# A fourth matmul group ahead of the first output, one product on GpSimd, and other unit widths, in an attention block fused with a mixture of experts

## Chip, cores and metric

The kernel runs on one core of a Trainium2 chip. The metric is the device time of one execution in microseconds; smaller is better. All data is float32 (the sketch matrices S1 and S2 arrive as float64 and are turned into float32 on the chip).

## What is computed

The first block is an attention with a sketched polynomial feature map; its output is the input x of a gated mixture of four experts.

```python
batch, n_heads, seq, head_dim = (4, 4, 1088, 32)   # r = 8
def phi(x):
    a = np.einsum('rd,bhsd->bhsr', S1, x)
    b = np.einsum('rd,bhsd->bhsr', S2, x)
    return np.einsum('bhsi,bhsj->bhsij', a, b).reshape(*x.shape[:-1], r * r)
q_p, k_p = (phi(q), phi(k))
kv = np.einsum('bhsf,bhsd->bhfd', k_p, v)
z = np.sum(k_p, axis=2)
num = np.einsum('bhsf,bhfd->bhsd', q_p, kv)
den = np.einsum('bhsf,bhf->bhs', q_p, z)[..., None] + 1e-06
x = num / den                              # laid out as 4352 rows of 128
...
p = domain_probs / (domain_probs.sum(-1, keepdims=True) + 1e-09)
for e in range(4):                         # F = 1024
    out += p[:, e:e+1] * (np.maximum(x @ w1[e], 0.0) @ w2[e])
```

## The kernel before

**Chunks and steps.** The 4352 columns of x (one per token, 128 partitions each, held in `xT`) are worked through in eleven chunks of 128, 448, 512 (six times), 320, 256 and 128 columns (`CHUNKS`; chunk 0 and the last are "plain"). A chunk has 16 steps, four for each expert, and steps are numbered through: step 16 is the first of chunk 1, step 48 the first of chunk 3. `first(i)` makes step i's hidden values: matmuls of `w1_sb` with `xT` into a bank `h` (three such banks, pool `ps_h`), a relu on ScalarE (ACT, L799 in a plain chunk, L807 otherwise) and, in chunks that aren't plain, rectify-and-subtract on VectorE (DVE, L778). Such a step has two halves j = 0 and 1, each with its own bank h, one L778 instruction in the first half and two in the second. `second(i)` multiplies the hidden values with the second weights into the banks `o0` and `o1`. The main loop issues `first(i)` and then `second(i - LA)` with LA = 2. After an expert's last step `gather` and `gather_rest` sum the output on ACT and GpSimd (POOL); `weight_sums` puts further sums on POOL up to step 28.

**Attention in pieces.** The attention of the 4 batches is cut into 275 pieces (`front`), which are put between the steps' halves by `work()`. A batch has first 19 pieces for its keys (`keys`: three turns kT, three projections kp0 to kp2 with copies by ACT, three copies of values by ACT together with the first of eight products `kp` on DVE (L383), two empty pieces, two key sums on PE, one block product), then 20 pieces for each unit of queries (`queries`: a turn qT, a projection qc into the bank `f`, shuffles and products on DVE giving qp, and `attend`: matmuls into the banks `den` and `num`, a reciprocal, a product xs, a turn y, and DMAs on SyncE's (SP) queue out to DRAM and back into xT). Units may have other widths than chunks; `UNITS` has them for each batch, and each batch has 1088 columns.

**Pacing.** `needed[m]` is the number of pieces after which all columns of chunk m have been issued. Before each step the rate of pieces is set to the largest over the chunks c ahead of

```python
(needed[c] + (8 if c > 1 else 4) - done[0]) / (START[c] - gone)
```

times the columns of a step. Each half adds half the rate to a credit, and a piece is issued for every whole credit.

**Start.** `start()` is written out by hand: keys of batch 0, the first unit of 128 columns by `attend_first` (banks `den` and `num`, into xT by L526), and the projection of the second unit. Key products there are shared between DVE (those with a `kf` argument read the bank in PSUM) and POOL (these read the copy `fs` in SBUF); key sums into `f`, `kvz` (L406) and the reciprocals follow. Then the h of steps 0 to 2 are begun on the first 64 columns of xT, while the second 64 are still made (`begun_hp`, `half_columns`).

Of the kernel before, what the change touches and what calls it, by code (L numbers as in the profile page):

```python
# [23 lines left out]
def kernel(  # L24
# [23 lines left out]
    nc = tc.nc  # L48

    P = 128  # L50
    HP = 64
# [10 lines left out]
    CW = 512  # L62
    GE = 160
    LA = 2
    UNITS = [[P, 448, 512], [512, 320, 256], [448, 512, P], [384, 320, 384]]

    CHUNKS = [P, 448, 512] + [512] * 5 + [320, 256, P]
    NC = len(CHUNKS)
# [10 lines left out]
    ps_n = ctx.enter_context(tc.tile_pool(name="ps_n", bufs=1, space=bass.MemoryType.PSUM))  # L79
# [3 lines left out]
    def psum(pool, tag):  # L83
        return pool.tile([P, 512], F32, tag=tag, name=tag)
# [217 lines left out]
    def load_gate(m, engine=nc.sync):  # L302
        gate[m] = mpool.tile([P, CW * E], F32, tag="gate", name="gate")
        for b, c, n, at in parts(m):
            engine.dma_start(
                gate[m][:, at * E : (at + n) * E], gates[b, c * E : (c + n) * E].partition_broadcast(P)
            )
# [72 lines left out]
    def key_product(b, t0, n, p, x, eng, kf=None):  # L380

        src, off = (kf, P * p) if kf is not None else (fss[b], 32 * (NT * p + t0))
        eng.tensor_tensor(  # L383
            out=_ap(kps[b], 0, P, 256 * t0 + P * p + 64 * x, [[256, n], [32, 2], [R, 4], [1, R]]),
            in0=_ap(src, 0, P, off + 4 * x, [[32, n], [R2, 2], [1, 4], [0, R]]),
            in1=_ap(fss[b], 0, P, 32 * (NT * p + t0) + R, [[32, n], [R2, 2], [0, 4], [1, R]]),
            op=ALU.mult,
        )
# [277 lines left out]
    def start():  # L666


        b, n = 0, UNITS[0][0]
        kf = []  # L670
        for t0 in (0, 2):
            key_turn(b, 0, t0, 2)
        for r in (1, 2):
            key_turn(b, r)
        qT = query_turn(b, 0, n)
        for gi in range(3):
            kf.append(psum(ps_h, "h"))
        value = value_copy(b)
        key_project(b, 0, kf[0])
        key_project(b, 1, kf[1])  # L680
        next(value)
        key_project(b, 2, kf[2])
        for _ in value:
            pass
        fq = [psum(ps_o, "o0"), psum(ps_o, "o1"), psum(ps_n, "num")]
        for i in range(3):
            for j in range(2):
                both(fq[i][:, 0:n], sr[:, i, j, :], qT[:, 0:n], start=(j == 0), stop=(j == 1))
        qb = apool.tile([P, QW], F32, tag="qb", name="qb")
        nc.scalar.copy(qb[:, 0:n], fq[0][:, 0:n])  # L690
        for x in range(2):
            key_product(b, 0, 4, 0, x, nc.vector, kf[0])
            key_product(b, 0, 4, 1, x, nc.gpsimd)
        for x in range(2):
            key_product(b, 4, 4, 0, x, nc.vector, kf[1])
            key_product(b, 8, 1, 0, x, nc.vector, kf[2])
        key_product(b, 4, 5, 1, 0, nc.gpsimd)
        key_product(b, 4, 4, 1, 1, nc.vector, kf[1])
        key_product(b, 8, 1, 1, 1, nc.vector, kf[2])
        kv = psum(ps_f, "f")  # L700
        for t0, n0 in ((0, 4), (4, 5)):
            for p in range(2):
                key_sum(b, p, kv, t0, n0)
        qp = query_tiles()
        for x in range(2):
            for p in range(2):
                query_product(qp, p, x, n, fq[1 + x], qb)
        for h in range(H):
            nc.gpsimd.tensor_copy(_ap(sq, 32 * h, 32, 32 * h, [[R2, 2], [1, R2]]), _ap(s_T, 0, 32, 0, [[D, 2], [1, R2]]))

        n1 = UNITS[b][1]
        qT = apool.tile([P, QW], F32, tag="qT2", name="qT2")
        turns = query_turns(b, n, n1, qT)
        next(turns)
        key_divide(b, kv)
        for _ in turns:
            pass
        first = attend_first(b, 0, n, qp)
        next(first)
        early[b, n] = psum(ps_o, "o1")  # L720
        both(early[b, n][:, 0:n1], sq[:, :], qT[:, 0:n1], start=True, stop=True)
        for _ in first:
            pass
        key_blocks(b, kv)
        gate_sums()

    def front():
        for b in range(B):
# [4 lines left out]
            c = 0  # L733
            for n in UNITS[b]:
                if b or c:
# [14 lines left out]
    def by_blocks(t, n, off=0):  # L750
        return _ap(t, 0, P, off, [[32, n // 32], [1, 32]])

    begun_hp = {}

    def half_columns(i, hp, c):

        e, f = divmod(i, NP)
        for j in range(2):
            both(
                hp[:, P * j + c : P * j + c + HP],  # L760
                w1_sb[:, e, P * (2 * f + j) : P * (2 * f + j + 1)],
                xT[:, c : c + HP],
                start=True,
                stop=True,
            )

    def first(i, work):

        m, kq = steps[i]
        n, (e, f) = CHUNKS[m], divmod(kq, NP)
        w = n // 2
        hd = mpool.tile([P, 4 * CW], F32, tag="hid", bufs=4, name="hid")
        hid[i] = hd

        def rectify_and_subtract(out, src, in1):
            nc.vector.scalar_tensor_tensor(out=out, in0=src, scalar=0.0, in1=in1, op0=ALU.max, op1=ALU.subtract)  # L778

        if plain(m):  # L780
            if i in begun_hp:
                hp = begun_hp.pop(i)
                half_columns(i, hp, HP)
            else:
                hp = psum(ps_h, "h")
                for j in range(2):
                    both(
                        hp[:, n * j : n * j + n],
                        w1_sb[:, e, P * (2 * f + j) : P * (2 * f + j + 1)],
                        xT[:, START[m] : START[m] + n],  # L790
                        start=True,
                        stop=True,
                    )
            if m and kq % 2:
                nc.vector.tensor_scalar(
                    out=hd[:, 0 : 2 * n], in0=hp[:, 0 : 2 * n], scalar1=0.0, scalar2=None, op0=ALU.max
                )
            else:
                nc.scalar.activation(hd[:, 0 : 2 * n], hp[:, 0 : 2 * n], ACTF.Relu)  # L799
            work()  # L800
            work()
            return
        for j in range(2):
            hp = psum(ps_h, "h")
            c = P * (2 * f + j)
            both(hp[:, 0:n], w1_sb[:, e, c : c + P], xT[:, START[m] : START[m] + n], start=True, stop=True)
            nc.scalar.activation(hd[:, n * j : n * j + n], hp[:, 0:n], ACTF.Relu)  # L807
            if j == 0:
                rectify_and_subtract(hd[:, 4 * w : 5 * w], hp[:, w:n], hd[:, 0:w])
            else:  # L810
                rectify_and_subtract(
                    _ap(hd, 0, P, 5 * w, [[w, 2], [1, w]]),
                    _ap(hp, 0, P, w, [[0, 2], [1, w]]),
                    _ap(hd, 0, P, w, [[3 * w, 2], [1, w]]),
                )
                rectify_and_subtract(hd[:, 7 * w : 8 * w], hp[:, 0:w], hd[:, 6 * w : 7 * w])
            work()
# [150 lines left out]
    for i in range(len(steps) + LA):  # L968
        if i < len(steps):
            m, kq = steps[i]  # L970
            while have[0] < START[m] + CHUNKS[m]:
                piece()

            gone = START[m] + CHUNKS[m] * kq / NQ
            rate = CHUNKS[m] / NQ * max([0] + [(needed[c] + (8 if c > 1 else 4) - done[0]) / (START[c] - gone) for c in range(m + 1, NC)])

            def work():

                if not NQ <= i < NQ + 2:
                    credit[0] = min(credit[0] + rate / 2, 2)  # L980
                while credit[0] >= 1:
                    credit[0] -= 1
                    piece()

            first(i, work)
            if i > NQ - 4:
                if i == NQ - 3:

                    nc.gpsimd.tensor_copy(behind[:, :], xT[:, START[2] - 1 : START[2]])
                next(to_sum, None)  # L990
            if i == 2:
                gate_quotients()
            elif i == 5:
                store_gates()
                load_gate(1)
                load_gate(2)
                load_batch(1)
            if m > 1 and kq == LA + 3 and m + 2 < NC:
                load_gate(m + 1)
        if i >= LA:  # L1000
            second(i - LA)
            mm, kk = steps[i - LA]
            if kk % NP == NP - 1 and not plain(mm):
                ending = chain(ending, gather(mm, kk // NP))
            else:
                next(ending, None)
# [29 lines left out]
```

## Time and profile before

| | |
|---|---|
| median of 4 runs | 488.06 us (487.82 to 488.31) |
| profiled execution, its own time | 487.82 us |
| span in the profile | 485.9 us |
| granted TensorE clock, mean | 1.000 |
| first matmul on xT, first output, first matmul of chunk 1 | 13.36, 15.02, 28.7 us |
| first matmul of chunk 2, of chunk 3 | 75.1, 130.8 us |
| last matmul starts | 482.3 us |

The span runs from the first to the last instruction of the program; the profiled execution's own time has 1.92 us around it. PE is TensorE's matmul, PEld its weight load, which overlaps. In a timeline a line has the start, the time from the first to the last of its instructions, the engine, the source line, the operation, its tiles, its shape and the count, and in brackets the idle time before it and what ended it. In the waits a line has who waited for whom: the sum, the times and the longest. A list by source line has the shortest, median and longest duration in ns.

### The profile page before, as it was taken

Reading aid. Unit: us, or ns where it says so; the run is one execution under the profiler, and the core shown is the slowest. Engines: PE = TensorE matmul, PEld = TensorE weight load, DVE = VectorE, ACT = ScalarE, POOL = GpSimd, SP = SyncE. Lnnn points to the kernel's source line nnn. Section 1 sums busy time; section 2 is a strip of 40 time slices with the busy share of each in tenths; the row PEclk is TensorE's granted clock in tenths of the full one; section 3 lists DMA queues with packets and bytes.
Section 4 is the critical chain, followed back from the end, with each engine's and each line's share of the span. In section 5 each row is a group of like instructions: output and inputs, shape, how many; then the busy total and the mean of one; then the engine's idle time right before and its main releaser. Section 6 shows DMA issues by size and latency. Waiting matters only on the chain.

```text
span 485.9 us, 11359 instructions
## 1 busy us (share of the span) xinstructions
PE 481.0 (99%) x4543; PEld 363.7 (75%) x4543; DVE 320.6 (66%) x760; ACT 246.8 (51%) x496; POOL 229.8 (47%) x269
## 2 busy tenths in 40 slices
PE   8999999999999999999999999999999999999997
PEld 6965666667777777777777777777777777999997
DVE  6859675686766668486776757668674676655642
ACT  4354564445544555355445555445455555566751
POOL 5172654435444455415455444514455446565570
PEclk9999999999999999999999999999999999999999
DMA  8890050211003123021103100021101200120000
GB/s 237 264 299 10 23 150 12 75 32 45 2 9 107 23 69 93 3 89 20 40 1 130 23 13 1 3 86 24 34 1 55 50 0 1 47 54 3 15 3 18
DMA packets 37588, 26.25 MB, mean 54 GB/s; under 512 B 24736, under 2 KB 34336, under 8 KB 37024
## 3 DMA queue, kind: packets, MB, share of 16 engines
q1 hardware_dynamic: 37520, 25.53, 18.9%
q8 instruction: 36, 0.59, 0.5%
q14 instruction: 16, 0.13, 0.1%
q10 hardware_dynamic: 16, 0.00, 0.0%
HBM read 21.28 MB, written 4.24 MB: 53 GB/s over the span
## 4 chain that ended last, share of the span: by engine, by line
PE 97%; DMA 1%; DVE 1%; issue 0%; SPq 0%; ACT 0%; ACTq 0%
PE h L194 50%; PE o L194 41%; PE f L194 3%; PE den L194 2%; DMA kn<-in_k_dram 1%; PE num L194 1%; DVE kp L383 0%; DVE qp L493 0%; DVE kT L320 0%; SPq L119 0%; DVE qT L480 0%; DVE end L846 0%; DVE kvz L406 0%; ACT fs L352 0%; ACTq L329 0%
## 5 line engine op out<-in xcount | busy, mean ns | idle before, releaser
L194 PE MATMUL h<-xT,w_sb 128*64 128x512 f32 (+5 forms) x1432 | 298.8, 490 | 0.0
L778 DVE SCALAR_TENSOR_TENSOR hid<-h,hid 128x256 f32<-128x256 f32 (+6 forms) x432 | 203.6, 472 | 143.4 <-ACT hid L807 134.5
L807 ACT ACTIVATE hid<-h 128x512 f32<-128x512 f32 (+3 forms) x288 | 158.5, 550 | 192.0 <-PE h L194 143.8
L194 PE MATMUL o<-hid,w2s 128*64 128x256 f32 (+3 forms) x1152 | 224.0, 355 | 0.0
L194 PEld LDWEIGHTS h<-xT,w_sb 128*64 128x64 f32 x1432 | 146.8, 137 | 49.7 <-issue 6.1
L194 PE MATMUL o<-hid,w_sb 128*64 128x256 f32 (+3 forms) x864 | 183.9, 355 | 0.0
L194 PEld LDWEIGHTS o<-hid,w2s 128*64 128x64 f32 x1152 | 132.3, 137 | 28.9
L922 POOL TENSOR_TENSOR ev<-yz,sh 64x256 f32<-64x256 f32 (+3 forms) x72 | 48.6, 674 | 159.8 <-ACT sh L925 157.1
L194 PEld LDWEIGHTS o<-hid,w_sb 128*64 128x64 f32 x864 | 100.7, 137 | 24.5 <-issue 5.2
L910 POOL TENSOR_TENSOR yz<-ev 128x512 f32<-128x512 f32 (+3 forms) x36 | 41.5, 1154 | 60.2 <-ACT ev L913 60.0
L922 POOL TENSOR_TENSOR ct<-ev 128x512 f32<-128x512 f32 (+3 forms) x36 | 42.5, 1181 | 2.8
L922 POOL TENSOR_TENSOR total<-total,ct 128x512 f32<-128x512 f32 (+3 forms) x27 | 32.2, 1194 | 2.1
L922 POOL TENSOR_TENSOR ct<-ct,gate 128x512 f32<-128x512 f32 (+3 forms) x27 | 31.8, 1177 | 2.1
L493 DVE TENSOR_TENSOR qp<-qa,qb 64x512 f32<-64x512 f32 (+5 forms) x44 | 30.0, 683 | 1.0
L912 ACT COPY ev<-o 128x512 f32<-128x512 f32 (+3 forms) x36 | 19.4, 539 | 12.7 <-PE o L194 12.3
L194 PE MATMUL o<-w_sb,hid 128*64 128x128 f32 x256 | 21.3, 274 | 0.0
L913 ACT COPY ev<-o 128x512 f32<-128x512 f32 (+3 forms) x36 | 19.4, 539 | 2.0
L194 PEld LDWEIGHTS o<-w_sb,hid 128*64 128x64 f32 x256 | 16.9, 137 | 1.8 <-issue 0.9
L799 ACT ACTIVATE hid<-h 128x256 f32<-128x256 f32 x24 | 8.8, 385 | 18.2 <-PE h L194 17.8
L383 DVE TENSOR_TENSOR kp<-fs 128x256 f32<-128x256 f32 (+1 forms) x24 | 16.4, 688 | 0.1
L925 ACT COPY sh<-yz 64x256 f32<-64x256 f32 (+3 forms) x36 | 13.7, 380 | 1.7 <-POOL yz L910 0.8
L194 PEld LDWEIGHTS den<-kvx,qp 128*64 128x64 f32 x240 | 12.2, 137 | 2.6 <-issue 0.5
(126 smaller groups left out, 244.4 us busy)
## 6 DMA issues: line engine op xcount, KB each, us to landing
w_sb<-in_moe_w_dram SPq DMA_DIRECT2D x8, 512.0 KB, 8.0
gate<-gates SPq DMA_DIRECT2D x4, 1024.0 KB, 5.4
kn<-in_k_dram SPq DMA_DIRECT2D x4, 544.0 KB, 4.0
vn<-in_v_dram SPq DMA_DIRECT2D x16, 128.0 KB, 2.9
gate<-gates SPq DMA_DIRECT2D x2, 896.0 KB, 5.1
qn<-in_q_dram SPq DMA_DIRECT2D x3, 544.0 KB, 5.1
out_dram<-ob SPq DMA_DIRECT2D x16, 64.0 KB, 2.0
xd<-y SPq DMA_DIRECT2D x14, 64.0 KB, 1.8
```

The lines of the kernel that those rows point to most:

```text
L194: nc.tensor.matmul(out(s), weights(s), moving(s), **flags)
L383: eng.tensor_tensor(out=_ap(kps[b], 0, P, 256 * t0 + P * p + 64 * x, [[256, n], [32, 2], [R, 4], [1, R]]), in0=_ap(src, 0, P, off + 4 * x, ...
L493: nc.vector.tensor_tensor(out=qp[p][64 * x : 64 * x + 64, 0:n], in0=qa[64 * p : 64 * p + 64, 0:n], in1=qb[64 * p : 64 * p + 64, 0:n], op=A ...
L778: nc.vector.scalar_tensor_tensor(out=out, in0=src, scalar=0.0, in1=in1, op0=ALU.max, op1=ALU.subtract)
L799: nc.scalar.activation(hd[:, 0 : 2 * n], hp[:, 0 : 2 * n], ACTF.Relu)
L807: nc.scalar.activation(hd[:, n * j : n * j + n], hp[:, 0:n], ACTF.Relu)
L910: add = lambda out, in0, in1, op=ALU.add: nc.gpsimd.tensor_tensor(out=out, in0=in0, in1=in1, op=op)
L912: nc.scalar.copy(_ap(ev, 0, P, 0, [[2 * w, 2], [1, w]]), _ap(a0, 0, P, 0, two))
L913: nc.scalar.copy(_ap(ev, 0, P, w, [[2 * w, 2], [1, w]]), _ap(a1, 0, P, 0, two))
L922: add = lambda out, in0, in1, op=ALU.add: nc.gpsimd.tensor_tensor(out=out, in0=in0, in1=in1, op=op)
L925: nc.scalar.copy(sh[HP:P, 0:w], yz[0:HP, 0, 0:w])
```

## The change

Three edits. The units of batches 1 and 2 (counted from 0) become 384, 384 and 320 columns. In `start()` one small key product (one tile, x = 1 of the second pair of heads) goes from DVE to POOL, and reads the copy `fs` instead of the bank. The matmuls of step 3 into h are issued at i = 2, ahead of `second(0)`, in two halves of 64 columns and into the bank `num`; `first(3)` then finds them made.

```diff
-    UNITS = [[P, 448, 512], [512, 320, 256], [448, 512, P], [384, 320, 384]]
+    UNITS = [[P, 448, 512]] + [[384, 384, 320]] * 2 + [[384, 320, 384]]
...
         key_product(b, 4, 5, 1, 0, nc.gpsimd)
+        key_product(b, 8, 1, 1, 1, nc.gpsimd)
         key_product(b, 4, 4, 1, 1, nc.vector, kf[1])
-        key_product(b, 8, 1, 1, 1, nc.vector, kf[2])
...
-    begun_hp = {}
+    begun_hp, made_hp = {}, {}
...
             if i in begun_hp:
                 hp = begun_hp.pop(i)
                 half_columns(i, hp, HP)
+            elif i in made_hp:
+                hp = made_hp.pop(i)
             else:
                 hp = psum(ps_h, "h")
...
+        if i == LA:
+
+            made_hp[3] = psum(ps_n, "num")
+            for c in (0, HP):
+                half_columns(3, made_hp[3], c)
         if i >= LA:
             second(i - LA)
```

## The prediction

> **What bounds the kernel now.** I read the page first, then the waits of TensorE (PE), then the timeline of the first 22 us, last VectorE (DVE) where it is busiest.
>
> ```profile
> PE 481.0 (99%) x4543; PEld 363.7 (75%) x4543; DVE 320.6 (66%) x760; ACT 246.8 (51%) x496; POOL 229.8 (47%) x269
> ...
> PE 97%; DMA 1%; DVE 1%; issue 0%; SPq 0%; ACT 0%; ACTq 0%
> ```
>
> PE is busy almost throughout and carries the chain. Busy PE need not be dense, so the waits:
>
> ```profile
> PE h L182 <- PEq L1020: 0.8, 1, 0.8
> PE h L194 <- DVE kT L320: 0.4, 1, 0.4
> PE den L194 <- DVE kvz L406: 0.3, 1, 0.3
> ```
>
> Those are all of PE's waits, and all lie before 12 us. From 28.7 us to the last matmul at 482 us the matmuls stand back to back. So a change can gain only in the first 16 us or by fewer matmul columns; in the middle it can only lose. The start:
>
> ```profile
> 8.78 1.15 DVE L383 TENSOR_TENSOR kp<-h,fs 128x64 f32<-128x64 f32 x5 [0.21 <-ACT fs L352]
> ...
> 11.06 0.45 DVE L480 STREAM_TRANSPOSE qT<-qn 128x256 f32<-128x256 f32 x1
> ...
> 11.54 0.49 DVE L406 TENSOR_TENSOR kvz<-f,own 128x128 f32<-128x128 f32 x2
> ...
> 11.88 0.44 PE L194 MATMUL den<-qp,kvz 128*64 128x128 f32 x4 [0.32 <-DVE kvz L406]
> ...
> 13.36 1.64 PE L194 MATMUL h<-xT,w_sb 128*64 128x64 f32 x48
> ...
> 15.02 0.42 PEld L194 LDWEIGHTS o<-w_sb,hid 128*64 128x64 f32 x8 [0.16 <-ACT hid L799]
> ...
> 20.86 0.62 DVE L493 TENSOR_TENSOR qp<-qa,qb 64x448 f32<-64x448 f32 x1
> ```
>
> DVE works without a break from 8.78 to the kvz that PE waits for, and PE waits again before the first output at 15.02.
>
> **Small product to GpSimd.** DVE loses one 128x64 product. The next instruction started 0.13 us after this one (9.716 to 9.847), so everything behind it moves up 0.13: four qp products, the turn at 11.06, kvz. The sums' last matmul ends at 11.35, and the hop from DVE to PE is 0.054 (xT's product ends at 13.308, its matmul starts at 13.362), so kvz at 11.41 is just allowed. On GpSimd the product costs about 0.3 (nearest row: a 128x68 sum, 0.30), behind the 0.74 product that ends at 9.56 and ahead of four copies into sq (9.50 to 10.48) that then end near 10.8; PE reads sq at 12.43, and reaches the last key sum near 11.0. Both are covered with over 1 us. Gain 0.13 (0 to 0.14).
>
> **Fourth step's hp in front of the first output.** It removes 8 matmuls of 128 columns from behind that output (436 ns, 15.507 to 15.943) and puts 16 of 64 columns ahead: 8 pairs at the 58 ns of the 48 matmuls at 13.36, 467 ns. They start where PE stood from 14.84 to 15.02, and the slow first pair (153 instead of 102 ns) goes too. The second output came at 15.94; now 14.84 - 0.13 + 0.47 + 0.44 = 15.61, so PE is 0.33 ahead. The num bank is free: its last reader ends at 14.03 and its next writer comes at 21.53, long after this step's ACT pass (0.39).
>
> **What takes part of it back.** At step 9 PE needs the qp product that ends at 21.48; PE loaded from it at 21.59, so 0.06 was spare. DVE runs unbroken from 14.1 to there and moves up only 0.13. PE therefore keeps 0.13 + 0.06 = 0.19 of its 0.33. What if the copies into xT that end at 27.8 stayed put? PE needs them at 28.7: no price. Start: -0.19 (-0.33 to 0).
>
> **Units.** PE's columns don't change. The attention's products are counted in tiles of 128: 4+3+2 and 4+4+1 before, 3+3+3 twice now, nine per batch both times; the qc columns are 1088 per batch. DVE loses six small bank instructions (0.15 to 0.3 each), which frees nothing on PE. What moves is the pace. Counting pieces by the planner's rule, chunk 3 (columns 1088 to 1600) needed 77 pieces and now needs 97, since the unit that ends at 1472 no longer covers it. Pieces per step go from (235 + 8 - 22) / 3008 x 28 = 2.06 to (97 + 8 - 22) / 960 x 28 = 2.42 at the start of chunk 1, and from 2.40 to 3.00 in chunk 2. In before, the eight key products of batch 1 lie one in each half step from 28 to 32; now they lie in steps 27, 27, 27, 28, 28, 29, 29, 29, two of them in one half twice, and the three value copies on ACT fall between the halves of step 27.
>
> ```profile
> 68.67 0.93 DVE L383 TENSOR_TENSOR kp<-fs 128x256 f32<-128x256 f32 x1
> 69.53 1.04 DVE L778 SCALAR_TENSOR_TENSOR hid<-h,hid 128x448 f32<-128x448 f32 x2
> 70.48 1.23 DVE L383 TENSOR_TENSOR kp<-fs 128x256 f32<-128x256 f32 x1
> 71.64 0.38 DVE L778 SCALAR_TENSOR_TENSOR hid<-h,hid 128x224 f32<-128x224 f32 x1
> ```
>
> The reader sees products of 0.93 and 1.23 that push the L778 behind them; that L778 frees a bank of h. There are three such banks, so PE wants each again three halves on. The last L778 above ended at 72.01, 0.65 late, and PE rewrote its bank at 72.82. An undelayed one in step 31 left 1.53.
>
> Now step 27, by those rows. In batch 2 three copies between two relus made the second 1.1 late, which eats the pause of about 1.0 that DVE has there. So the first L778 of step 28 is late by the two products P2 + P3 plus 0.14, against a room of 1.38 after the hop: PE waits P2 + P3 - 1.24. P4 and P5 follow before the first L778 of step 29: two steps without attention take 5.66 us, 3.0 of them between these two L778, and DVE's own work in between is 1.55 (0.37 + 0.95 + 0.23); the room there is 1.36 (68.75 to 70.17 in step 29), so PE has waited P2 + P3 + P4 + P5 - 2.68 by then. From there the key sums (1.04 us of PE) give room. What is a product?
>
> ```profile
> L383 DVE TENSOR_TENSOR kp<-fs x24: 406/501/1485, 67.0 to 306.8; 128x256 f32<-128x256 f32 x12, 128x320 f32<-128x320 f32 x12
> L383 DVE TENSOR_TENSOR kp<-h,fs x8: 215/414/424, 7.2 to 9.7; 128x256 f32<-128x256 f32 x5, 128x64 f32<-128x64 f32 x3
> ```
>
> From PSUM never over 0.42, from SBUF up to 1.49: the long ones lie beside GpSimd's work. By the groups' means (0.65 and 0.73, 0.06 of each overlapped) four make 2.44: no wait. By contended rows (a pair back to back at 299.67 took 2.02, 1.94 to the next start; single ones held DVE 0.86 at 68.67 and 0.72 at 187.25) they make 3.5: a wait of 0.84. By the longest spacing, 1.16 each, 1.96. GpSimd's gather of chunk 1 (ev, ct, ct, total, each 0.7 to 1.2) starts behind step 27's second relu and so beside them; I take 0.6, nearer the contended end. Range 0 to 1.96.
>
> The Trainium skill ("SBUF — State Buffer", Who interferes with whom) speaks against packing these products: a VectorE instruction with two SBUF inputs and a GpSimd one that reads SBUF exclude each other for a whole instruction. Taken strictly, each of four products would wait out one GpSimd instruction of about 1.1 and add its 0.41, an estimate of some 6 us in sum and 3.3 of waiting; the rows don't show each product paying that.
>
> Two smaller places. The turn of unit (1,384) now follows y in half 38, and its qc comes in half 39. Counted from the step's start, DVE is done at about 4.9 (L778 at 2.75 + 1.07, y 0.5, turn 0.6) and PE is there at 4.93: 0 to 0.3, I take 0.05. And chunk 3's columns now leave in step 45 instead of 42: y about 2.25 after the step's start (143.45 against 141.2), 3.6 until the read back is issued, 3.2 to land, so 9.05; PE needs them after three steps and one qc, 10.2. That leaves 1.2: covered, and SP has nothing that waits ahead of it there. If that cover goes, every us of delay beyond it is a us.
>
> **Sum.** -0.19 + 0.60 + 0.05 = +0.46. The profiled execution took 487.82, with a span of 485.9 and 1.92 around it; it lies 0.24 under the median, so the sum gives 488.3 against it and **488.5** against the median 488.06. About 0.2%, or 0.98 us, is what a measurement can tell from no change.
>
> **Rivals.**
> - Slower: packed products. If DVE's products in steps 27 to 29 sit beside GpSimd all the way, PE waits 1.2 to 2.0 there. It decides from 1.12 us of waiting on, that is when the four take over 3.8 us. Time 489.1 to 490.1. For: the pair of 2.02. Against: only some products are long. Chance 0.27. Its sibling, the landing of chunk 3, gives the same times when DVE or SP is 2.3 us late at step 45: 0.10.
> - Covered: the products are short, no wait, and the start alone counts: 487.73 to 488.0. For: the means. Chance 0.24.
> - Not doing what it says: hp fills PE but the step 9 wait eats all, with no loss elsewhere: 488.06. Chance 0.07.
> - Faster: an unseen 1 us. PE waits under 1.6 us in all, and only 0.33 is in reach of the change. 487.0. Chance 0.06.
>
> **How the numbers follow.** My forecast, a wait between, has 0.26 (488.2 to 489.0). Within 0.2%: 0.26 + 0.24 + 0.07 = 0.57; slower 0.37; faster 0.06. The range 487.6 to 490.0 runs from the covered case to the upper bound of the packed products; what is left out is the faster case and the far end of the slower ones.
>
> **What would show it.** Right: kvz starts near 11.41; hp's 16 matmuls stand from 14.7 to 15.2 and the wait on ACT at the first output is gone; a new wait of PE (or its weight loads) on DVE hid L778 near 66 to 72 us, nothing near chunk 3's start at about 132. Wrong: a wait on a DMA of xT, products of 0.4 throughout, or a count of matmuls that changes other than by h's 8 more.

## The result, and the profile after

| | before | after |
|---|---|---|
| median | 488.15 us (52 runs, 487.57 to 489.00) | 489.02 us (32 runs, 488.43 to 489.87) |
| profiled execution, its own time and span | 487.82, 485.9 us | 489.02, 487.2 us |
| first matmul on xT, step 4's h, chunk 1 | 13.36, 16.38, 28.71 us | 13.23, 16.05, 28.91 us |

The ratio is 1.0017, with a 95% interval of 1.0013 to 1.0022: about 0.83 us slower, 0.63 to 1.07 by the interval. Medians and ratios here and below leave out the few runs with a granted clock far under 1 or a time far above all others; the profiled execution of one experiment (hp alone) was such a run, at 0.753, and is not read.

The page after, busy time and the chain that ended last:

```profile
PE 482.2 (99%) x4551; PEld 368.9 (76%) x4551; DVE 319.9 (66%) x753; ACT 246.9 (51%) x496; POOL 230.5 (47%) x270
...
PE 96%; DVE 2%; DMA 1%; issue 0%; ACT 0%; SPq 0%; ACTq 0%
```

PE has the 8 more matmuls that hp was to bring (4543 to 4551), DVE seven instructions less and POOL one more. DVE's share of the chain went from 1% to 2%. All waits of PE's matmuls, who waited for whom, sum, times, longest:

```profile
PE h L182 <- PEq L1027: 0.8, 1, 0.8
PE h L194 <- DVE hid L778: 0.3, 1, 0.3
PE h L194 <- DVE kT L320: 0.2, 1, 0.2
PE den L194 <- DVE kvz L406: 0.2, 1, 0.2
```

Three lie in front of 12 us as before. The one on L778 is new. The timeline of PE and of its weight loads there:

```profile
69.97 0.92 PE L194 MATMUL h<-xT,w_sb 128*64 128x448 f32 x3
71.17 0.97 PE L194 MATMUL h<-xT,w_sb 128*64 128x448 f32 x4 [0.29 <-DVE hid L778]
```
```profile
71.17 0.20 PEld L194 LDWEIGHTS h<-xT,w_sb 128*64 128x64 f32 x4 [1.06 <-DVE hid L778]
```

The bracket of 0.29 understates it, since the end of a matmul is modelled. By the starts: the array's two halves began their last matmuls at 70.00 and 70.34, and 0.38 later each could have begun the next; both began at 71.17. That is 0.79 and 0.45 lost, 0.62 in the mean. Who was late is in DVE's timeline (start, time, engine, line, operation, count):

```profile
64.71 1.05 DVE L778 SCALAR_TENSOR_TENSOR hid<-h,hid 128x448 f32<-128x448 f32 x2 [1.08 <-ACT hid L809]
65.68 1.29 DVE L383 TENSOR_TENSOR kp<-fs 128x256 f32<-128x256 f32 x2
66.89 0.38 DVE L778 SCALAR_TENSOR_TENSOR hid<-h,hid 128x224 f32<-128x224 f32 x1
67.20 1.06 DVE L383 TENSOR_TENSOR kp<-fs 128x256 f32<-128x256 f32 x1
68.18 1.04 DVE L778 SCALAR_TENSOR_TENSOR hid<-h,hid 128x448 f32<-128x448 f32 x2
69.13 0.21 DVE L378 TENSOR_TENSOR fs<-num,fs 128x64 f32<-128x64 f32 x1
69.38 1.44 DVE L383 TENSOR_TENSOR kp<-fs 128x320 f32<-128x320 f32 x1
70.74 0.38 DVE L778 SCALAR_TENSOR_TENSOR hid<-h,hid 128x224 f32<-128x224 f32 x1
```

From 65.68 on DVE has no pause. Its four products take 1.29 (the first two together), 1.06 and 1.44, where the same work alone takes 0.41 to 0.49 each, and the L778 that frees PE's bank ends at 71.12. The chain in front of it is ACT's: the three copies of values stand between the two relus (L809) of step 27, and so the L778 at 64.71 is late, which eats DVE's pause:

```profile
62.33 0.54 ACT L809 ACTIVATE hid<-h 128x448 f32<-128x448 f32 x1 [1.54 <-issue]
62.90 1.15 ACT L329 COPY vx<-vn 128x512 f32<-128x512 f32 x2
63.95 0.29 ACT L334 COPY vx<-vn 64x128 f32<-64x128 f32 x1
64.14 0.53 ACT L809 ACTIVATE hid<-h 128x448 f32<-128x448 f32 x1
```

And beside the products GpSimd gathers chunk 1's output, without a pause:

```profile
65.22 1.46 POOL L924 TENSOR_TENSOR ev<-yz,sh 64x224 f32<-64x224 f32 x2 [4.33 <-ACT sh L927]
66.77 1.20 POOL L924 TENSOR_TENSOR ct<-ev 128x448 f32<-128x448 f32 x1
68.05 1.21 POOL L924 TENSOR_TENSOR ct<-ct,gate 128x448 f32<-128x448 f32 x1
69.33 1.14 POOL L924 TENSOR_TENSOR total<-total,ct 128x448 f32<-128x448 f32 x1
```

The start, DVE's timeline and then the chain in order of time:

```profile
8.78 1.02 DVE L383 TENSOR_TENSOR kp<-h,fs 128x64 f32<-128x64 f32 x4 [0.21 <-ACT fs L352]
...
11.41 0.49 DVE L406 TENSOR_TENSOR kvz<-f,own 128x128 f32<-128x128 f32 x2
```
```profile
14.87 0.47 PE num L194 x16
15.34 0.88 PE o L194 x16
16.22 0.44 PE h L194 x8
...
20.14 0.12 issue
20.26 0.32 PE h L194
```

kvz begins at 11.41. hp's 16 matmuls into num take 0.47 us of the chain; by their starts they begin at 14.70, the first output follows at 15.17, and the wait on ACT in front of it (0.16 before) is gone. The h of step 4 begins at 16.05 instead of 16.38: 0.33 ahead, to the hundredth as worked out. Then, at 20.26, PE breaks off inside step 8's h. No semaphore is named ("issue"), the matmul comes 0.40 late, the two halves of the array run out of step until about 28.5, and chunk 1 begins 0.20 later than before instead of 0.19 earlier.

**Where the 1.3 us of span lie.** For PE's time after 29 us I set each matmul's columns against the pace of an unbroken stretch (on one half of the array a matmul of 128 columns follows another after 0.109 us, one of 448 after 0.376) and summed what is lost: 0.35 us before, 1.44 after. The level hangs on the exact pace by some 0.2, the difference of 1.09 hardly. It has 0.66 at 71.2, 0.17 between 46 and 68 us, where the key projections now lie, and 0.26 in small parts. One of the waits between 46 and 68 has a name, among those of PE's weight loads:

```profile
PEld f L194 <- DVE kT L320: 0.5, 1, 0.5
```

At 55.13 the first key projection of batch 1 loads DVE's turn kT, which ended at 55.07; by the starts one half of the array lost 0.1 there, 0.05 in the mean. With the start's 0.20 the difference makes 1.29.

That is more than the 0.87 between the medians, since the profiled execution of the kernel before, 487.82, is itself 0.33 under its median. The profiles hold one execution each; where they and the medians differ, the medians say what the change costs.

### The profile page after: what moved, and what is told of

Read it like the earlier page. It is cut to its first block, busy times and chain, and to the rows that moved or that the text cites. A ratio compares the mean times of both kernels' runs of the same rounds, so it can differ in the third digit from the quotient of the medians.

```text
span 487.2 us, 11369 instructions
## 1 busy us (share of the span) xinstructions
PE 482.2 (99%) x4551; PEld 368.9 (76%) x4551; DVE 319.9 (66%) x753; ACT 246.9 (51%) x496; POOL 230.5 (47%) x270
## 4 chain that ended last, share of the span: by engine, by line
PE 96%; DVE 2%; DMA 1%; issue 0%; ACT 0%; SPq 0%; ACTq 0%
PE h L194 49%; PE o L194 40%; PE f L194 3%; PE den L194 2%; DMA kn<-in_k_dram 1%; DVE kp L383 1%; DVE hid L778 1%; PE num L194 0%; DVE qp L493 0%; DVE kT L320 0%; ACT hid L809 0%; DVE qT L480 0%; SPq L119 0%; DVE end L848 0%; DVE kvz L406 0%
## 5 line engine op out<-in xcount | busy, mean ns | idle before, releaser
L778 DVE SCALAR_TENSOR_TENSOR hid<-h,hid 128x256 f32<-128x256 f32 (+6 forms) x432 | 203.7, 472 | 145.2 <-ACT hid L809 136.4
L809 ACT ACTIVATE hid<-h 128x512 f32<-128x512 f32 (+3 forms) x288 | 158.4, 550 | 193.7 <-PE h L194 152.3
L194 PEld LDWEIGHTS h<-xT,w_sb 128*64 128x64 f32 x1424 | 149.7, 137 | 49.4 <-issue 4.4
L912 POOL TENSOR_TENSOR yz<-ev 128x512 f32<-128x512 f32 (+3 forms) x36 | 42.5, 1180 | 58.9 <-ACT ev L915 58.9
L493 DVE TENSOR_TENSOR qp<-qa,qb 64x384 f32<-64x384 f32 (+3 forms) x44 | 30.9, 701 | 1.1
L194 PE MATMUL o<-w_sb,hid 128*64 128x128 f32 x256 | 22.3, 273 | 0.0
L194 PEld LDWEIGHTS o<-w_sb,hid 128*64 128x64 f32 x256 | 18.1, 137 | 1.6 <-issue 0.9
L383 DVE TENSOR_TENSOR kp<-fs 128x256 f32<-128x256 f32 (+1 forms) x24 | 15.0, 633 | 0.1
L194 PEld LDWEIGHTS den<-kvx,qp 128*64 128x64 f32 x264 | 13.3, 137 | 2.2 <-issue 0.2
```

Source lines behind the costliest of these rows:

```text
L194: nc.tensor.matmul(out(s), weights(s), moving(s), **flags)
L383: eng.tensor_tensor(out=_ap(kps[b], 0, P, 256 * t0 + P * p + 64 * x, [[256, n], [32, 2], [R, 4], [1, R]]), in0=_ap(src, 0, P, off + 4 * x, ...
L493: nc.vector.tensor_tensor(out=qp[p][64 * x : 64 * x + 64, 0:n], in0=qa[64 * p : 64 * p + 64, 0:n], in1=qb[64 * p : 64 * p + 64, 0:n], op=A ...
L912: add = lambda out, in0, in1, op=ALU.add: nc.gpsimd.tensor_tensor(out=out, in0=in0, in1=in1, op=op)
```

## The experiments

All are compared with the kernel before on the same chip. PE's loss at L778 and the loss after 29 us are worked out as above, from each run's one profile.

| kernel | median us | ratio, 95% interval | at L778 near 71 | loss after 29 us |
|---|---|---|---|---|
| before (four chips) | 488.07 to 488.25 | 1 | none | 0.35 |
| after | 489.02 | 1.0017, 1.0013 to 1.0022 | 0.62 | 1.44 |
| the start's edits alone | 487.98 | 0.9997, 0.9988 to 1.0006 | none | 0.65 |
| units alone | 488.92 | 1.0018, 1.0009 to 1.0027 | yes | 1.42 |
| batch 1's units alone | 488.94 | 1.0020, 1.0011 to 1.0029 | yes | 1.50 |
| after, copies earlier | 488.16 | 1.0002, 0.9993 to 1.0011 | none | 0.68 |
| after, one gather left out | 488.25 | 1.0002, 0.9994 to 1.0011 | none | 0.68 |
| after, batch 1's old units | 488.36 | 1.0006, 0.9997 to 1.0015 | 0.3 | 0.85 |
| hp alone | 488.29 | 1.0005, 0.9995 to 1.0014 | not read | not read |
| product alone | 488.13 | 1.0002, 0.9993 to 1.0011 | none | 0.67 |
| start's edits, weights first | 488.45 | 1.0004, 0.9995 to 1.0014 | none | 0.64 |
| start's edits, half the weights | 487.90 | 0.9992, 0.9983 to 1.0001 | none | 0.70 |
| start's edits, copies earlier | 487.84 | 0.9990, 0.9981 to 0.9999 | none | 0.35 |
| product, copies earlier | 487.75 | 0.9992, 0.9983 to 1.0001 | none | 0.35 |

**The start's edits alone, the units alone, batch 1's units alone.** The first is the changed kernel with

```diff
-    UNITS = [[P, 448, 512]] + [[384, 384, 320]] * 2 + [[384, 320, 384]]
+    UNITS = [[P, 448, 512], [512, 320, 256], [448, 512, P], [384, 320, 384]]
```

the second the kernel before with the opposite edit, and the third the kernel before with

```diff
-    UNITS = [[P, 448, 512], [512, 320, 256], [448, 512, P], [384, 320, 384]]
+    UNITS = [[P, 448, 512], [384, 384, 320], [448, 512, P], [384, 320, 384]]
```

> The kernel before with the two edits at the start (step 3's h in front of the first output, the small product on GpSimd) and the units of before. My theory: the start gains 0.19 us and nothing is lost later, so 0.2 us under before (488.0 beside 488.15), with kvz at 11.41 us and chunk 1 starting near 28.5 instead of 28.7. Rival: running ahead makes TensorE break off near 20 us every time (0.4 us, as in the profile after), so that the start loses 0.2: 488.35, chunk 1 near 28.9.

> The kernel before with the new units alone. My theory: key products packed beside GpSimd in chunk 1 make TensorE wait for a bank of h by 0.7 to 0.8 us near 71 us, so 0.8 to 1.1 over before (488.95 to 489.25). Rival: the units cost nothing and the loss is in the start: 488.15, no wait on L778.

> Only batch 1 gets 384, 384, 320; batch 2 keeps 448, 512, 128. My theory: chunk 3 sets the pace of chunks 1 and 2 and the whole loss is batch 1's: within 0.2 us of the units alone (488.9 to 489.25), with the same wait near 71 us. Rival: both batches lose alike, by more small losses along the run: about 0.4 us over before (488.55).

The units carry the whole loss (1.0018 without the start's edits, 1.0017 with them), and those of batch 1 alone carry it (1.0020). In batch 1's alone DVE's products take 1.29, 1.06 and 1.45, within 0.01 of those after. By the medians the start's edits are worth 0.09 us (488.07 to 487.98), which the interval (0.6 us faster to 0.3 slower) does not tell from nothing. In the profile kvz begins 4.19 us after the first key product, as forecast, but chunk 1 begins at 28.80 and not near 28.5. It shows a wait that the prediction had not priced: step 4's h comes upon expert 1's first weights, 0.41 us late by the starts.

```profile
16.43 0.66 PE L194 MATMUL h<-xT,w_sb 128*64 128x128 f32 x8 [0.24 <-DMA w_sb<-in_moe_w_dram]
```

**Is it ACT's copies or the products' length?** Two kernels take away one each. The first is the changed kernel with the value copies one piece earlier, together with the third projection and not with the first product:

```diff
                 key_add(b, gi - 1, kf[gi - 1])
+            if gi == 2:
+                for _ in value_copy(b):
+                    pass
             yield
-        for _ in value_copy(b):
-            pass
```

> The kernel after, with ScalarE's three value copies issued one piece earlier (with the last key projection, at the end of step 26 instead of between the halves of step 27). My theory: the lateness that the copies bring (about 1.1 us) goes, VectorE is no longer late enough, and the wait of 0.8 us for the bank of h goes: 488.2 to 488.4 against 489.0 of after. Rival: the products beside GpSimd alone make VectorE late: the wait stays at 0.5 to 0.8 us and the time at 488.8 to 489.0.

Measured: 488.16, no wait on L778. DVE's timeline (this kernel's L779 is L778):

```profile
63.32 1.05 DVE L779 SCALAR_TENSOR_TENSOR hid<-h,hid 128x448 f32<-128x448 f32 x2
64.29 1.28 DVE L383 TENSOR_TENSOR kp<-fs 128x256 f32<-128x256 f32 x2
65.61 0.39 DVE L779 SCALAR_TENSOR_TENSOR hid<-h,hid 128x224 f32<-128x224 f32 x1
...
69.33 0.38 DVE L779 SCALAR_TENSOR_TENSOR hid<-h,hid 128x224 f32<-128x224 f32 x1
```

The products are as long as after (1.28 for the pair), but they start 1.39 earlier (some 0.3 of it since chunk 1 begins that much earlier in this execution), and so the L778 that mattered starts at 69.33 instead of 70.74. The pause that the late relu had eaten is enough to carry them. The second kernel leaves the copies and takes away what GpSimd does beside the products, for one expert of one chunk:

```diff
+        if (m, e) == (1, 1):
+            yield
+            return
         add(ev[HP:P, 0:w], yz[HP:P, 0, 0:w], sh[HP:P, 0:w])
```

> The whole change, but GpSimd's four groups of additions and products for expert 1 of chunk 1 are left out (that expert's share of these 448 columns is missing from the output), so that GpSimd stands still from about 65.2 to 70.4 us. The three copies of values stay between the halves of step 27. Theory (DVE's key products become long because they lie beside GpSimd, and their length with the late second relu is the wait): the four products take about 0.41 to 0.5 each, their spacings 0.35 to 0.45, so P2+P3+P4+P5-2.68 is about -1.1: the wait of 0.8 at about 71 is gone, and the time falls by 0.7 to 0.9 against the whole change, to about 488.1. Rival (the late second relu alone makes the wait, the products' length is not in it): the wait stays at 0.5 or more and the time stays near 489.0. Rival (two products packed in one half are too much at any length): the wait stays, 489.0.

Measured: 488.25, no wait on L778. DVE's timeline:

```profile
65.05 1.05 DVE L778 SCALAR_TENSOR_TENSOR hid<-h,hid 128x448 f32<-128x448 f32 x2 [1.08 <-ACT hid L809]
66.02 0.75 DVE L383 TENSOR_TENSOR kp<-fs 128x256 f32<-128x256 f32 x2
66.68 0.38 DVE L778 SCALAR_TENSOR_TENSOR hid<-h,hid 128x224 f32<-128x224 f32 x1
66.98 0.41 DVE L383 TENSOR_TENSOR kp<-fs 128x256 f32<-128x256 f32 x1
...
68.52 0.49 DVE L383 TENSOR_TENSOR kp<-fs 128x320 f32<-128x320 f32 x1
68.93 0.38 DVE L778 SCALAR_TENSOR_TENSOR hid<-h,hid 128x224 f32<-128x224 f32 x1
```

L778 is as late at first (1.08 of waiting on ACT), but the pair takes 0.75 instead of 1.29, the others 0.41 and 0.49. So the wait at 71 us needs both: the late relu and GpSimd beside the products. Either one taken away gives back 0.77 to 0.86 us, the whole loss within the intervals (some 0.4 us each way). Two products in one half, which both kernels keep, make no wait there by themselves.

**Batch 2's units.** The changed kernel with batch 1's row of `UNITS` as before (512, 320, 256).

> The whole change, but batch 1 keeps its units of 512, 320 and 256 columns; batch 2 has 384, 384 and 320. Theory (batch 1's units alone cost the time): no wait of PE on L778 near 71 and a time as with the start's edits alone, 487.8 to 488.1, ratio to before 0.9995 to 1.0003. Rival (batch 2's units have a part in the loss): 488.3 or more, and lost time of PE after 130 us that the kernel before does not have.

Measured: 488.36, above the 487.8 to 488.1 of the theory that batch 1's units alone matter, though the interval (0.9997 to 1.0015) reaches below 1, so the time alone tells it neither from that theory nor from no change. The profile tells more: the rate of pieces is the largest over all chunks ahead, so batch 2's units quicken batch 1's pieces too, and now another pair falls into one half:

```profile
70.76 2.25 DVE L383 TENSOR_TENSOR kp<-fs 128x320 f32<-128x320 f32 x2
72.94 0.38 DVE L778 SCALAR_TENSOR_TENSOR hid<-h,hid 128x224 f32<-128x224 f32 x1
```

This pair lies beside GpSimd too, and PE lost 0.30 at 73.4, its only loss on L778 there. Whether a late relu has a part in it was not tested. Batch 1's units are enough for the whole loss; by this one profile batch 2's are not free of it.

**The start: product alone, hp alone, the weights.** The product alone is the kernel before with this edit, and hp alone the kernel with the start's edits and this edit undone:

```diff
         key_product(b, 4, 5, 1, 0, nc.gpsimd)
+        key_product(b, 8, 1, 1, 1, nc.gpsimd)
         key_product(b, 4, 4, 1, 1, nc.vector, kf[1])
-        key_product(b, 8, 1, 1, 1, nc.vector, kf[2])
```

> Only the small product on GpSimd; h of step 3 stays behind the first output and the units are those of before. By the prediction's working kvz starts 4.20 us after the first key product of the start (4.33 before) and all behind it moves up with it: chunk 1 starts 15.68 us after the first product into xT as before, time 487.93. Since PE gains only 0.13, its 345th matmul stays over 2.7 us behind the start of the second block of instructions, and nothing breaks off. Rival (the 0.13 is lost before 28 us): chunk 1 15.8 us or more after the product into xT, 488.1.

> Only step 3's h ahead of the first output; the product stays on DVE and the units are those of before. By the prediction's own working PE is then 0.33-0.13 = 0.20 ahead at the second output, the kvz does not move, and the wait on step 9's qp product leaves 0.06: from the first product into xT to chunk 1 15.62 us against 15.68 before, time 488.0. Rival (the landing of expert 1's first weights is met): PE breaks off for a w_sb load near 16.5, 15.9 us or more, time 488.1 to 488.4.

The product does what was worked out: kvz begins 4.20 us after the first key product (4.33 before), and chunk 1 begins 15.69 us after the first product into xT (15.68 before). In time this 0.13 is below what can be told (a ratio of 1.0002, with one run of 490.38 among the 12; the medians on that chip are 488.25 and 488.13). hp alone has no readable profile, and its time (1.0005) tells nothing either; it is inconclusive.

The next two ask why hp's lead did not last. In the first the weights of experts 0 and 1 go ahead of the small loads of the probabilities; in the second, whose expectation says what it leaves out, half of the weights are not loaded.

```diff
     load_w1(0)
+    load_w2(0)
+    load_w1(1)
...
-    load_w2(0)
-    for e in range(1, E):
+    load_w2(1)
+    for e in range(2, E):
```

> The units of before, both edits of the start, and the loads of expert 0's second and expert 1's first weights issued ahead of the small loads of the domain probabilities instead of behind them. In the profile with the start's edits alone PE broke off 0.4 us at 16.43 for expert 1's first weights. Theory (hp puts PE ahead of that landing, which takes back what the start wins): no wait on a w_sb load, chunk 1 starts 15.6 us after the first product into xT (15.96 with the start's edits alone, 15.68 before), time 487.7, 0.2 to 0.4 under the start's edits alone. Rival (the landing is only met in some executions and is worth nothing in the median): 487.95 to 488.05, as with the start's edits alone. Rival (the probabilities now come later and GpSimd's sums on them hold up its copies): a wait on POOL or later copies into xT, over 488.2.

```diff
-    for e in range(1, E):
+    for e in range(1, 2):
         load_w1(e)
...
-                w1_sb[:, e, P * (2 * f + j) : P * (2 * f + j + 1)],
+                w1_sb[:, e % 2, P * (2 * f + j) : P * (2 * f + j + 1)],
```

> The units of before and both edits of the start, but the weights of experts 2 and 3 are not loaded: experts 0 and 1 are used in their place (so the output is that of other weights), and 2 MB less lie in the DMA queues between 10 and 24 us. In nine profiles TensorE's second 16 KB block of instructions began to come in at 17.25 to 18.87 us, and where the 345th matmul was due earlier than 2.5 to 2.65 us after that, PE broke off there (four of the six with hp ahead, by 0.3 to 0.47). Theory (the block is late because it lies behind the weights): it begins well before 17 us, the landing of expert 1's first weights is not met either, nothing breaks off between 13 and 28 us but the 0.08 for step 9's qp product, and chunk 1 starts 15.61 us after the first product into xT (15.68 before); time 487.8. Rival (the block is asked for when PE gets to a certain instruction, whatever the DMA queues hold): it begins at 17 to 18 us as ever and the break at the 345th matmul comes as often; chunk 1 15.9 to 16.0 us after the product, 488.0 to 488.4.

With the weights first they land at 14.97 and step 4 no longer waits for them, but nothing is won: PE breaks off at 20.31 by 0.47 us instead. (The median, 488.45, lies where the rival with late probabilities has it, over 488.2, but PE's waits name nothing of the kind, and the interval takes in no change.) That break always hits the same matmul, the 345th (counted from 0). The traces have DMA packets of 16 KB of kind "instruction", 36 in the span, one for about 252 of PE's 9086 matmuls and weight loads, so I take them for PE's instructions; the second begins at 16 to 19 us. For each readable profile, in the order of the distance from the packet's begin to that matmul's start ("late by" is the mean of the array's two halves, against 0.109 us from matmul to matmul):

| kernel | packet begins | 345th matmul | distance | late by | xT's first product to chunk 1 |
|---|---|---|---|---|---|
| start's edits, copies earlier | 17.81 | 20.24 | 2.43 | 0.12 | 15.74 |
| after, batch 1's old units | 17.70 | 20.17 | 2.47 | 0.34 | 15.96 |
| batch 1's units alone | 18.87 | 21.39 | 2.52 | 0.09 | 16.39 |
| start's edits, weights first | 17.76 | 20.31 | 2.55 | 0.47 | 16.09 |
| after, one gather left out | 18.00 | 20.60 | 2.60 | 0.28 | 16.21 |
| after | 17.62 | 20.26 | 2.64 | 0.40 | 16.01 |
| after, copies earlier | 17.25 | 19.99 | 2.74 | 0 | 15.61 |
| start's edits alone | 17.43 | 20.27 | 2.84 | 0 | 15.96 |
| product alone | 17.66 | 20.61 | 2.95 | 0 | 15.69 |
| units alone | 17.57 | 20.77 | 3.20 | 0 | 15.68 |
| product, copies earlier | 17.28 | 20.50 | 3.22 | 0 | 15.67 |
| before | 17.31 | 20.64 | 3.33 | 0 | 15.68 |
| start's edits, half the weights | 15.90 | 21.18 | 5.28 | 0 | 16.56 |

Every matmul that came under 2.65 us behind the packet was late, and none of the others: five of the eight profiles with hp, and one of the five without. Before, there were 0.7 us to spare, and hp's lead of 0.33 with a packet some 0.3 later uses them up. With half the weights the packet begins at 15.90, 1.35 earlier than in any other, as the theory has it that it lies behind them in the DMA queues. The median, 487.90, is near the theory's 487.8, but the interval takes in no change, and the profiled execution was the slowest of the 11 (488.99): its forecast of 15.61 us from xT to chunk 1 failed. By the starts PE lost 0.39 there on expert 1's first weights, at 17.34, and 0.51 at 14.74, on a matmul that was late in no other profile and again with no semaphore named:

```profile
14.74 0.92 PE L194 MATMUL h<-xT,w_sb 128*64 128x64 f32 x24 [0.34 <-issue]
...
17.34 0.66 PE L194 MATMUL h<-xT,w_sb 128*64 128x128 f32 x8 [0.19 <-DMA w_sb<-in_moe_w_dram]
```

That one is the 219th, 126 matmuls ahead of the 345th. The first packet began at 12.32 there, later than in any other profile, and the matmul came 2.42 us behind it; in the other twelve it came 2.44 us or more behind its packet and was on time. This fits the same cause, one packet earlier. It also means that fewer weights did not make both packets early: that the weights delay the second one rests on this one profile. And that the late matmuls lacked their instructions is inferred from the order of these distances; no run here moved the place of the break.

The Trainium skill ("Runtime: NRT & Kernel Launch", Instruction fetch mechanics) says that the instructions are refilled in blocks of 16 KiB while the current one is executed, and that crossing into the next is mostly hidden. The sizes agree. If these breaks are such crossings, then here, with the weights coming in at the same time, the one at the 345th matmul was hidden in seven profiles and cost up to 0.47 us in six.

**A version under both.** The start's edits, or the product alone, with the units of before and the copies one piece earlier:

> The units of before, both edits of the start, and the three copies of values one piece earlier in every batch. The aim is a version under both kernels. Theory: the copies' earlier place takes the late relu from in front of the key products, so that the small waits on L778 that some executions of the kernel before show (0.25 to 0.3 near 73 or 305 us) do not come; lost time of PE after 29 us 0.3 or less and a time of 487.7 to 488.0. Rival (the middle has nothing to give with these units, and the start gives under 0.1): 488.0 to 488.2. Rival (the copies now push key additions or relus elsewhere): 488.3 or more, with a new wait on L778 or a later first key product.

> The units of before, the small product on GpSimd and the three copies of values one piece earlier, but h of step 3 behind the first output as before; the twin of the version with both edits of the start, which stood at a ratio of 0.999 to before. Theory (hp is worth nothing or less, since PE then runs into its second block of instructions and its two sides fall out of step until 28 us; the product's 0.13 is kept): chunk 1 starts 15.68 us after the first product into xT, the 345th matmul comes 2.75 us or more after that block begins to come in and does not break off; ratio to before 0.9988 to 0.9996. Rival (hp is worth the 0.06 to 0.2 that the prediction gave it, and breaks are rare in executions without a profile): a ratio 0.0002 to 0.0004 above that of its twin, 0.9992 to 0.9998. The two ranges overlap, so the time alone will not decide; the profile shows whether the start behaves as with the product alone.

Both have no wait on L778, lose 0.35 after 29 us, and stand at 0.9990 and 0.9992; only the first one's interval (0.9981 to 0.9999) lies below 1, by a hair and as the only one of the experiments to do so, so a gain over the kernel before is likely rather than shown. Against the changed kernel they are about 1.2 us faster. What the copies' place gives with the old units lies near 305 us, in batch 3's key products: in four of the profiles with the units of before (the start's edits alone, the product alone, and both with other loads) one product that began 0.007 to 0.016 us after a GpSimd instruction took 1.61 us, and PE lost 0.2 to 0.3 behind it; in the kernel before the same product began 0.005 us after it, took 0.49 in its one profile, and nothing was lost. Its other executions may well lose it, which would account for most of the 0.33 between that profile and the median; this is not shown. With the copies earlier the product took 0.49 in both. The waits of PE with the product and the copies earlier, all before 12 us:

```profile
PE h L182 <- PEq L1021: 0.8, 1, 0.8
PE den L194 <- DVE kvz L406: 0.2, 1, 0.2
PE h L194 <- DVE kT L320: 0.2, 1, 0.2
```

In this profile the start goes as forecast (15.67 us, 3.22 behind the packet), while its twin with hp broke off by 0.12. The times do not tell the two apart, so whether hp is worth anything at all stays open; of the profiles with hp, one of eight came to chunk 1 sooner after xT than before (by 0.07), and seven later, by 0.06 to 0.88.

## Why the prediction was right, and where it was not

The time, 489.02, is inside the range (487.6 to 490.0), 0.02 above the forecast case (488.2 to 489.0) and 0.08 short of the rival of packed products. That it fell inside owes something to a range 2.4 us wide: the sum of terms was 0.46 and the medians moved by 0.87. By the medians of the experiments the units cost 0.85 (0.65 forecast) and the start's edits gain 0.09 (0.19 forecast). The central mechanism, DVE's products beside GpSimd that hold up a bank of h, is the one that the runs show. Point by point:

- **Small product:** right. kvz at 11.41 as said; 0.13 in every profile that has the edit but the one with half the weights, where the turn in front of kvz waited 0.19 for the DMA of qn. PE's waits name neither GpSimd's product nor its copies into sq.
- **hp:** right in size as far as 16 us (0.33 ahead), wrong after it. The step that failed is the one on what takes the lead back: it named one wait, on step 9's qp product. That wait is there where nothing else is (0.08 at 21.5 in the changed kernel with the copies earlier, where hp's gain behind xT was 0.07 against the 0.06 worked out). But two obstacles lie in front of it that the prediction did not look for: the landing of expert 1's weights near 16.4 (met in two of the eight profiles with hp), and the break at the 345th matmul near 20.2 (met in five), which I put down to PE's own instructions. Instead of -0.19 the profile has +0.20, and the medians of the start's edits alone about -0.1.
- **The wait on the bank:** right in place, cause and size: 0.60 said, 0.62 to 0.66 lost at 71.2. The working holds step by step. From the starts of the lines after, P2 + P3 is 1.21, P4 0.98 and P5 1.36; P2 + P3 - 1.24 is no wait at the first bank, and none came there; P2 + P3 + P4 + P5 - 2.68 is 0.87, against the 0.79 of the half of the array that lost more. The prediction's reading by contended rows (3.5 in sum, a wait of 0.84) hit it; the step down to 0.6 was hedging, and came out only because the array's other half lost less.
- **The strict reading of the Trainium skill's rule** ("SBUF — State Buffer", Who interferes with whom) was mis-sized, and this was the best lead on offer. In the traces before and after, 19 of the 48 products on DVE from SBUF took over 0.55 us; all 19 began while a GpSimd instruction ran, and each ended 0.28 to 0.35 us behind that instruction's end, whatever its own start. So the rule holds, but a product waits out the rest of the running instruction, not the whole of one, and once. As an estimate, half of GpSimd's 1.1 and 0.3 make 0.85 for a product, four make 3.4, and 3.4 - 2.68 is 0.72: that could have been worked out from before's trace, which has 11 of the 19. The prediction took a whole instruction each (3.3 of waiting) and then laid the rule aside.
- **qc of unit (1,384), chunk 3's landing:** neither shows a wait of PE. The 0.05 did not come. Chunk 3's columns were there in time: y was done at 125.5, the read back was issued at 128.6, and PE began on chunk 3 at 132.8 without a pause.
- **Not priced:** 0.17 between 46 and 68 us and 0.26 in small parts, over before. The first appears in the changed kernel with the copies earlier and in the one with the gather left out as well, in each with the weight load that waits 0.53 for the turn kT (55.1 after, 54.8 and 55.5 there); that is 0.05 of it, and the cause of the rest stays open. "Back to back" from 28.7 to 482 was nearly right: by this reckoning the kernel before loses 0.35 there.

By terms, in the profile: start 0.39 over the forecast, wait 0.06 over, qc 0.05 under, not priced 0.43: 0.83, and the sum came out at 1.29 instead of 0.46. This holds for the two profiled executions; between the medians it is 0.87.

## What to carry to other kernels

When units or pieces change size, count where the planner now puts each instruction, and look for two things falling together: a late producer (here three copies between two relus) and long neighbours (here GpSimd beside two-input products from SBUF). For a product beside a busy GpSimd, reckon the rest of the running GpSimd instruction plus 0.3 us, not the mean of all products. And where an edit lets the busiest engine run ahead, walk the whole lead down to the next thing that arrives at a time of its own: weights, and probably the engine's own instructions, as well as the operand that comes to mind first.

## What the runs showed of the hardware

- A DVE product of two SBUF operands, begun while a GpSimd instruction runs, ends 0.28 us (256 columns) or 0.35 (320) behind the end of that instruction; begun in a gap it takes 0.41 or 0.49. One that began 0.005 us after a GpSimd instruction took 0.49, and the same one 1.61 where it began 0.007 to 0.016 us after it. Two in a row beside GpSimd took 2.25 us.
- PE seems to run out of instructions without branches: the 345th matmul was late by 0.09 to 0.47 us in six of thirteen profiles, always when it came within 2.65 us of the begin of the second 16 KB packet, and the 219th by 0.51 in one, 2.42 us behind the first packet, while the weights were still coming in. The profile's only sign is "issue" as what ended the wait, and the array's halves out of step afterwards.
